# Linear attention with RMS norm and a SiLU feed-forward: other starting addresses for TensorE's operands

## The chip, the cores and the metric

One core of a Trainium2 chip. The metric is the device time of one execution in microseconds. The engines are TensorE (PE in the profile, its weight loads PEld), VectorE (DVE), ScalarE (ACT), GpSimd (POOL) and SyncE (SP), which issues all loads and stores here. A matmul on TensorE has two operands in the on-chip memory (SBUF): the stationary one, which it loads into its array ahead of the product, and the moving one, which it streams through it. Results go to PSUM.

## The reference

```python
kv  = einsum('bhsd,bhse->bhde', k, v)            # b 8, h 8, s 576, d 64
out = einsum('bhsd,bhde->bhse', q, kv)
x   = out / sqrt(mean(out * out, -1) + 1e-6) * g_norm
x   = x.transpose(0, 2, 1, 3).reshape(4608, 512)
h   = x @ w_in                                   # 512 x 2048
y   = (h / (1 + exp(-h))) @ w_out                # 2048 x 512
```

All in float32.

## The kernel before

The 4608 tokens are taken in nine tiles of 512 (t = 0 to 8), the 2048 hidden features in sixteen blocks of 128 (f). The attention of a batch element b (576 tokens, four pairs of heads) is done while TensorE works on the tile before the one that needs it, in jobs that are hung on fixed steps of the tile loop (`first_jobs`, `mid_jobs`, `last_jobs`). The order of all instructions is the order in which the program is written; nothing is rescheduled.

A float32 product is made of three products of rounded parts: each operand is an upper and a lower part (`gh` and `gl`, `wi[:, 0]` and `wi[:, 1]`, `qh` and `ql`), and lower by lower is left out. Nearly every matmul thus has a 128x128 stationary operand and 256 moving columns:

- `products` (through `halves`, line 479) makes the hidden layer of tiles 0 and 1: `wi` parts are stationary, x (`x_part`) moves. It writes `hp`.
- `product` (line 645) does the same for tiles 2 to 8, where a scheme of Strassen and Winograd's kind makes a pair of blocks from seven products. Stationary are `wi` parts or sums of them, moving are `x_second`, `operand4`, `operand5`, `operand6`. A pair of blocks takes 42 matmuls in two stretches, 24 and 18, that mostly follow each other.
- `project` (through `halves`, line 479) is the second layer: `gh` and `gl` are stationary, `w_out` parts (`wo`) move. It writes `acc` and, for a quarter of the last tile, `at`. A block f takes 24 matmuls, a pair 48.
- `mm_out` (lines 290 to 294) multiplies q by the state: `kh` and `kl` (or `kvm` in the plain form for b < 2) are stationary; q, or `qh` and `ql`, moves. It is done in two halves of the 576 tokens.
- `mm_kv` (line 257) makes the state from k (stationary) and v (moving), 64 columns at a time.

`pair_step` does a pair of blocks in tiles 2 to 8: 42 product matmuls, then the 48 project matmuls of the pair before. The q products of the next batch element stand between them in the first steps of a tile, four pairs of heads in two halves each; the k-v products stand in one block late in it.

Tiles live in pools. `const`, `weights`, `kvq`, `tmp`, `opool`, `small` and `gp` follow each other in SBUF in this order, and a pool gives its places out in the order in which the tags are first asked for. So a small unused tile (a "gap") at the head of a pool moves all behind it. In `weights`, places go to the tags `wo0` to `wo15` and `wi0` to `wi15`; at the start some of them hold k, v and q of the first batch element (`early`). `spare` and `late` give places in `const`: `x0` to `x2`, later `operand4` to `operand6` and the parts of the sums; and `x3`, `x32` and `wo_full`.

Of the kernel before, what the change touches and what calls it, by code (L numbers as in the profile page):

```python
# [8 lines left out]
F32 = mybir.dt.float32  # L9
# [21 lines left out]
def linear_attention_rms_silu_ffn(  # L31
# [23 lines left out]
    B, NP, P, S = q.shape  # L55
    D = P // 2
    DM = NP * P
    NF = w_in.shape[0]
    TN = 512
    NT = B * S // TN  # L60
    HS = S // 2
    LAG = 2
    WARM = 2

    const = ctx.enter_context(tc.tile_pool(name="const", bufs=1))
    weights = ctx.enter_context(tc.tile_pool(name="weights", bufs=1))
    kvq = ctx.enter_context(tc.tile_pool(name="kvq", bufs=8))
# [3 lines left out]
    gp = ctx.enter_context(tc.tile_pool(name="gp", bufs=LAG + 1))  # L71
# [2 lines left out]
    ps_at = ctx.enter_context(tc.tile_pool(name="ps_at", bufs=1, space=PSUM))  # L74
    dram = ctx.enter_context(tc.tile_pool(name="dram", bufs=1, space=bass.MemoryType.DRAM))

    gp.tile([P, 16], F32, name="gap_before_gated", bufs=1)
    kvm = [const.tile([P, P], F32, name=f"kvm{i}") for i in range(NP)]
    for t in kvm:
        nc.gpsimd.memset(t, 0.0)  # L80
# [4 lines left out]
    for i in range(4):  # L85
        nc.gpsimd.tensor_copy(
            out=both[32 * i:32 * i + 32, 32 * (i ^ 1):32 * (i ^ 1) + 32], in_=ident[32 * i:32 * i + 32, 32 * i:32 * i + 32]
        )


    warm_up = const.tile([P, 1], F32, name="warm_up")
    nc.gpsimd.memset(warm_up, 1.0)
    gcol = const.tile([P, 1], F32, name="gcol")
    d_eps = const.tile([P, 1], F32, name="d_eps")
    nc.gpsimd.memset(d_eps, float(D) * EPS)
    const.tile([P, 8], F32, name="gap")

    def load_g():
        for h in range(P // D):
# [7 lines left out]

    SHIFT = 48
    const.tile([P, SHIFT], F32, name="gap_before")
    x_second = const.tile([P, NP, 2, TN], F32R, name="x_second")
    x_first, lates = {}, {}

# [1 line left out]
        return const.tile(shape, dtype, name=name, tag=f"spare{n}")  # L118

    def late(n, shape, dtype, name):  # L120
        if not lates:
            const.tile([P, 64 - SHIFT], F32, name="gap_behind")
        if name not in lates:
            lates[name] = const.tile(shape, dtype, name=name, tag=f"late{n}")
        return lates[name]

    def x32(c, w):

        return late(c // 2, [P, 2, TN], F32, f"x32_{c // 2}")[:, c % 2, w]


    def block(kind, f, dtype):
        return weights.tile([P, 2, NP * P], dtype, name=f"{kind}{f}", tag=f"{kind}{f}")

    def load_block(kind, f):
        words[kind, f] = t = block(kind, f, I32)
        src = w_in.bitcast(I32)[f] if kind == "wi" else w_out.bitcast(I32)[f * P:(f + 1) * P, :]
        nc.sync.dma_start(out=t.rearrange("p a b -> p (a b)"), in_=src)
# [5 lines left out]
    def full_tile(kind, f):  # L144
        if kind == "wo":
            t = late(1, [P, 2, NP * P], F32, "wo_full")[:, f % 2]
        else:
            t = tmp.tile([P, S], F32, name="full", tag="tmp")[:, :NP * P]
        fulls[kind, f] = t
        return t  # L150
# [40 lines left out]
    def split_block(kind, f, upper):  # L191
        full = fulls.pop((kind, f))
        parts[kind, f] = w = block(kind, f, F32R)
        upper(out=w[:, 0, :], in_=full)
        nc.gpsimd.tensor_tensor(out=w[:, 1, :], in0=full, in1=w[:, 0, :].bitcast(F32), op=ALU.subtract)  # L195
# [9 lines left out]
    def x_part(t, a, c):  # L205

        if t == 1:
            return x_second[:, c, a]
        if c not in x_first:
            kind = {"shape": [P, 2, TN], "dtype": F32R, "name": f"x{c}"}  # L210
            x_first[c] = spare(c, **kind) if c < 3 else late(0, **kind)
        return x_first[c][:, a]
# [20 lines left out]
    class Pair:  # L233
# [50 lines left out]

        def mm_out(self, half):

            self.w = w = slice(half * HS, (half + 1) * HS)
            self.ps = ps = at_bank()[:, :HS]
            if self.plain:
                nc.tensor.matmul(out=ps, lhsT=self.kvm, rhs=self.q[:, w], start=True, stop=True)  # L290
                return
            nc.tensor.matmul(out=ps, lhsT=self.kh, rhs=self.ql[:, w], start=True, stop=False)  # L292
            nc.tensor.matmul(out=ps, lhsT=self.kl, rhs=self.qh[:, w], start=False, stop=False)  # L293
            nc.tensor.matmul(out=ps, lhsT=self.kh, rhs=self.qh[:, w], start=False, stop=True)  # L294
# [174 lines left out]
    def at_bank(tag=None):  # L469

        at_tags.append(at_tags.pop(0))
        return ps_at.tile([P, 512], F32, name="at", tag=tag or at_tags[-1])
# [101 lines left out]
    def place(name, n, dtype):  # L574

        if name not in once:
            once[name] = block("wi", HF + 2 * n + 1, dtype).rearrange("p a (j n) -> p a j n", n=H)
        return once[name]
# [235 lines left out]
    with tc.manual_schedule():  # L814
# [4 lines left out]
        for item in ORDER.split():  # L819
            kind, n = item.rstrip("0123456789"), int(item.lstrip("wiopbg") or 0)  # L820
# [236 lines left out]
```

## Time and profile before

| | |
|---|---|
| median of 3 runs | 841.53 us (841.49 to 841.56) |
| the profiled execution | 841.74 us, its span 840.0 us |
| PE busy | 830.0 us, 99% of the span, 7518 records |
| DVE, ACT, POOL busy | 63%, 43%, 17% |
| DMA | 122.81 MB, queue q1 at 41.5% of 16 engines |

A profile row names a group by line, engine and operation, and by the tiles that it writes and reads (`acc<-wo,gh` writes `acc`, the moving operand is `wo`, the stationary one `gh`). "Busy" counts overlapping instructions once; the mean is of single instructions, from start to end, and longer than the spacing of two, since they are pipelined. The chain of waits that ended last is followed back from the end; where it stays on one engine it gives, for each stretch of equal work, start, duration and count, and the duration over the count is the spacing. Some rows of the program appear as several in the trace: a matmul on plain float32 data does.

### The profile page before, as it was taken

How to read it: one execution, taken by the hardware profiler on the slowest of the kernel's cores; microseconds unless marked ns; L12 is line 12 of the kernel's file. 1: busy time of each engine (PE TensorE's matmuls, PEld its weight loads, DVE VectorE, ACT ScalarE, POOL GpSimd, SP SyncE). 2: the span in 40 equal slices, each digit the busy share in tenths (PEclk: the TensorE clock that was granted, in tenths of full speed). 3: DMA queues.
4: the chain of work that ended last, by engine and by line, in shares of the span. 5: the costliest groups of instructions: out<-in, count | busy, mean ns of one | idle time of the engine just before them, and what ended most of it. 6: DMA issues, size and time to landing. Idle time of an engine off the chain costs nothing.

```text
span 840.0 us, 18181 instructions
## 1 busy us (share of the span) xinstructions
PE 830.0 (99%) x7518; PEld 823.1 (98%) x7518; DVE 529.3 (63%) x1027; ACT 358.5 (43%) x744; POOL 146.0 (17%) x142
## 2 busy tenths in 40 slices
PE   9989999999999999999999999999999999999998
PEld 8889999999999999999999999999999999999998
DVE  4886875888376567657666667656865664464332
ACT  4766554534453255325542355235532432243222
POOL 2776883423020002000200011001100000000000
PEclk9999999999999999999999999999999999999999
DMA  8779011337342634364424452444423342334331
GB/s 330 304 257 363 2 58 52 141 140 271 99 174 93 219 109 153 101 214 144 165 98 155 162 171 88 157 158 157 151 96 105 102 151 102 101 101 151 101 101 51
DMA packets 42435, 122.81 MB, mean 146 GB/s; under 512 B 4849, under 2 KB 5105, under 8 KB 42353
## 3 DMA queue, kind: packets, MB, share of 16 engines
q1 hardware_dynamic: 42352, 121.65, 41.5%
q8 instruction: 59, 0.97, 0.5%
q14 instruction: 24, 0.19, 0.1%
HBM read 103.81 MB, written 17.83 MB: 145 GB/s over the span
## 4 chain that ended last, share of the span: by engine, by line
PE 94%; DMA 4%; POOL 1%; issue 0%; ACT 0%; SPq 0%
PE acc L479 47%; PE hp L645 32%; PE hp L479 9%; PE at L257 2%; DMA wo<-in_moe_w_out 1%; DMA k<-in_k 1%; DMA v<-in_v 1%; PE at L293 1%; PE at L294 1%; PE at L292 1%; DMA early_wi<-in_v 1%; PE at L479 1%; DMA wi<-in_moe_w_in 1%; PE at L290 1%; POOL wo L195 0%
## 5 line engine op out<-in xcount | busy, mean ns | idle before, releaser
L479 PE MATMUL acc<-wo,gh 128*128 128x256 f32 x2272 | 360.8, 281 | 0.0
L479 PEld LDWEIGHTS acc<-wo,gh 128*128 128x128 f32 x2272 | 307.3, 189 | 1.0 <-POOL wo L195 0.3
L479 PE MATMUL acc<-wo,gl 128*128 128x256 f32 x1136 | 226.8, 280 | 0.5 <-POOL gl L498 0.5
L479 PEld LDWEIGHTS acc<-wo,gl 128*128 128x128 f32 x1136 | 174.1, 189 | 0.7 <-POOL gl L498 0.7
L645 PE MATMUL hp<-x_second,wi 128*128 128x256 f32 x1344 | 163.7, 277 | 0.0
L645 PEld LDWEIGHTS hp<-x_second,wi 128*128 128x128 f32 x1344 | 158.0, 188 | 0.0
L645 PE MATMUL hp<-operand,wi 128*128 128x256 f32 x1008 | 124.7, 277 | 0.0
L645 PEld LDWEIGHTS hp<-operand,wi 128*128 128x128 f32 x1008 | 119.9, 188 | 0.0
L279 POOL TENSOR_TENSOR ql<-q,qh 128x576 fp32r<-128x576 f32 x24 | 35.6, 1485 | 377.2 <-ACT qh L278 342.6
L696 ACT COPY wi<-hp 128x256 f32<-128x256 f32 x56 | 20.9, 373 | 143.0 <-PE hp L645 143.0
L654 ACT ACTIVATE gh<-gf 128x512 fp32r<-128x512 f32 x56 | 35.4, 633 | 93.5 <-DVE gf L709 80.4
L654 ACT ACTIVATE gh<-wi 128x512 fp32r<-128x512 f32 x56 | 35.5, 634 | 80.5 <-DVE wi L709 67.6
L697 DVE TENSOR_TENSOR gf<-hp,wi 128x256 f32<-128x256 f32 x28 | 11.9, 425 | 86.4 <-ACT wi L696 86.4
L697 DVE TENSOR_TENSOR wi<-hp,wi 128x256 f32<-128x256 f32 x28 | 11.9, 425 | 85.8 <-ACT wi L696 85.8
L479 PE MATMUL hp<-x,wi 128*128 128x256 f32 x360 | 46.4, 283 | 1.5 <-POOL wi L195 1.5
L479 PE MATMUL hp<-x_second,wi 128*128 128x256 f32 x384 | 46.7, 278 | 0.0
L479 PEld LDWEIGHTS hp<-x,wi 128*128 128x128 f32 x360 | 43.3, 188 | 2.4 <-POOL wi L195 1.7
L658 DVE TENSOR_TENSOR gl<-wi,gh 128x512 fp32r<-128x512 f32 x56 | 38.4, 686 | 11.1 <-ACT wi L655 11.1
L479 PEld LDWEIGHTS hp<-x_second,wi 128*128 128x128 f32 x384 | 45.3, 188 | 0.1
L658 DVE TENSOR_TENSOR gl<-gf,gh 128x512 fp32r<-128x512 f32 x56 | 39.1, 698 | 7.4 <-ACT gf L655 7.4
L698 DVE TENSOR_TENSOR wi<-hp,wi 128x256 f32<-128x256 f32 x56 | 23.9, 426 | 29.8 <-PE hp L645 29.8
L320 DVE SCALAR_TENSOR_TENSOR x<-o,gcol,yT 128x128 f32<-128x128 f32 (+7 forms) x52 | 40.8, 784 | 1.9
(142 smaller groups left out, 997.7 us busy)
## 6 DMA issues: line engine op xcount, KB each, us to landing
wi<-sums_in_dram SPq DMA_DIRECT2D x112, 512.0 KB, 3.3
out<-ob SPq DMA_DIRECT2D x35, 256.0 KB, 2.2
wi<-in_moe_w_in SPq DMA_DIRECT2D x16, 512.0 KB, 7.6
wo<-in_moe_w_out SPq DMA_DIRECT2D x16, 512.0 KB, 8.5
sums_in_dram<-sum_parts SPq DMA_DIRECT2D x16, 512.0 KB, 2.9
k<-in_k SPq DMA_DIRECT2D x28, 288.0 KB, 4.7
v<-in_v SPq DMA_DIRECT2D x28, 288.0 KB, 5.2
q<-in_q SPq DMA_DIRECT2D x28, 288.0 KB, 3.8
```

Of the source, the lines that this page charges most:

```text
L257: nc.tensor.matmul(out=self.kv[h], lhsT=self.k[rows, c, :], rhs=self.v[rows, c, :], start=(start and r == 0), stop=(stop and r == 4),)
L279: nc.gpsimd.tensor_tensor(out=self.ql, in0=self.q, in1=self.qh.bitcast(F32), op=ALU.subtract)
L290: nc.tensor.matmul(out=ps, lhsT=self.kvm, rhs=self.q[:, w], start=True, stop=True)
L292: nc.tensor.matmul(out=ps, lhsT=self.kh, rhs=self.ql[:, w], start=True, stop=False)
L320: nc.vector.scalar_tensor_tensor(out=to, in0=self.o[:, a:e], scalar=gcol, in1=self.yT, op0=ALU.mult, op1=ALU.mult)
L479: nc.tensor.matmul(out=to[:, at:at + 256], lhsT=stationary, rhs=moving[:, at:at + 256], start=start and at == 0, stop=stop and at == n - 256,)
L645: nc.tensor.matmul(out=out, lhsT=a_of(i, a, c), rhs=x[:, b, c], start=(n == 0), stop=(n == 5))
L654: nc.scalar.activation(out=gh, in_=x, func=AF.Silu)
L658: nc.vector.tensor_tensor(out=gl, in0=x, in1=gh.bitcast(F32), op=ALU.subtract)
L696: nc.scalar.copy(out=p1, in_=u)
L697: nc.vector.tensor_tensor(out=c1[:, low], in0=v, in1=p1, op=ALU.add)
L698: nc.vector.tensor_tensor(out=u2, in0=y, in1=p1, op=ALU.add)
```

## The change

It moves data in SBUF and nothing else, but for one cut. Gaps of other sizes stand at the head of `const`, `kvq` and `gp`; one stands between `w_out`'s and `w_in`'s places in `weights`, and `weights_places` asks for all places of that pool in a fixed order before anything else is loaded. The halves of q's 576 columns become 256 and 320 instead of 288 and 288, so that the second begins 1024 bytes behind the first and not 1152.

```diff
-    HS = S // 2
+    CUT = 256
...
-    gp.tile([P, 16], F32, name="gap_before_gated", bufs=1)
+    def gap(pool, size, name):
+        pool.tile([P, size // 4], F32, name=name, bufs=1)
+
+    def weights_places():
+        for kind in ("wo", "wi"):
+            for f in range(NF):
+                block(kind, f, F32)
+            if kind == "wo":
+                gap(weights, 64, "gap_weights")
+
+    gap(const, 128, "gap_first")
+    gap(kvq, 192, "gap_q")
+    gap(gp, 64, "gap_gated")
...
-    const.tile([P, 8], F32, name="gap")
+    gap(const, 96, "gap_x")
...
-    SHIFT = 48
-    const.tile([P, SHIFT], F32, name="gap_before")
...
-        if not lates:
-            const.tile([P, 64 - SHIFT], F32, name="gap_behind")
...
+    weights_places()
...
-            self.w = w = slice(half * HS, (half + 1) * HS)
-            self.ps = ps = at_bank()[:, :HS]
+            self.w = w = (slice(0, CUT), slice(CUT, S))[half]
+            self.ps = ps = at_bank()[:, :w.stop - w.start]
```

Where the operands of TensorE begin, in bytes modulo 256, as the pools give the addresses out in the two programs (the steps inside these tiles are multiples of 256 bytes; the matmuls are the program's, not the trace's records):

| matmuls | count | moving, before | stationary, before | moving, after | stationary, after |
|---|---|---|---|---|---|
| `project`: wo by gh, gl | 3456 | 0 | 64 | 192 | 0 |
| `product`: x_second, operand4 to 6 by wi | 2352 | 192 | 0 | 192 | 0 |
| `products`: x0 to x2, x_second by wi | 672 | 192 | 0 | 192 | 0 |
| `products`: x3 by wi | 96 | 0 | 0 | 192 | 0 |
| q by kh, kl or kvm, first half | 76 | 0 | 128 | 192 | 0 |
| q by kh, kl or kvm, second half | 76 | 128 | 128 | 192 | 0 |
| k-v, b of 1 and more | 280 | 0 | 0 | 192 | 192 |
| k-v, first batch element | 40 | 0 | 0 | 0 and 192 | 192 and 0 |

No instruction is added or removed, and none changes its place on its engine or its waits; the q products and ACT's two copies of each are 256 and 320 columns wide.

## The prediction

> **What bounds the kernel now.** I read the page's busy times first, then its groups, then the chain of waits stage by stage, and the timeline of single blocks last.
>
> ```profile
> span 840.0 us, 18181 instructions
> PE 830.0 (99%) x7518; PEld 823.1 (98%) x7518; DVE 529.3 (63%) x1027; ACT 358.5 (43%) x744; POOL 146.0 (17%) x142
> PEclk9999999999999999999999999999999999999999
> ...
> L479 PE MATMUL acc<-wo,gh 128*128 128x256 f32 x2272 | 360.8, 281 | 0.0
> L645 PE MATMUL hp<-x_second,wi 128*128 128x256 f32 x1344 | 163.7, 277 | 0.0
> ```
>
> TensorE is busy for 99% of the span at the full granted clock, with no idle time ahead of its large groups; the next engine, DVE, stands at 63%. So the kernel is as long as its stream of matmuls, and only the time from one matmul's start to the next one's can move it. The two groups have one shape (128x128 weights, 256 columns) but means of 281 and 277 ns. These overlap; the spacing is what counts, and the chain of waits gives it, as a block's time over its count (columns: start, us, what):
>
> ```profile
> 212.53 2.63 PE at L257 x80
> ...
> 215.95 2.24 PE hp L479 x19
> 218.19 5.66 PE acc L479 x48
> 223.84 4.78 PE hp L645 x42
> 228.62 2.83 PE acc L479 x24
> ...
> 248.95 2.06 PE acc L479 x18
> 251.01 0.13 PE at L292
> ...
> 251.41 2.07 PE acc L479 x18
> ...
> 253.86 1.41 PE acc L479 x12
> 255.28 4.78 PE hp L645 x42
> 260.06 5.65 PE acc L479 x48
> ...
> 301.79 2.63 PE at L257 x80
> 304.41 5.66 PE acc L479 x48
> 310.07 4.95 PE hp L645 x42
> ```
>
> Line 645, `product`, mostly takes 4.78/42 = 113.8 ns a matmul; line 479 into `acc`, `project`, takes 5.65/48 = 117.7. But neither is bound to its number: the product block at 310.07 takes 4.95/42 = 117.9, and the project block at 304.41 is fast once it has started, as the timeline shows (two windows, rows of 4 and 2 matmuls in turn):
>
> ```profile
> 260.60 0.64 PE L479 MATMUL acc<-wo,gh 128*128 128x256 f32 x4
> ...
> 264.84 0.64 PE L479 MATMUL acc<-wo,gh 128*128 128x256 f32 x4
> 305.15 0.62 PE L479 MATMUL acc<-wo,gh 128*128 128x256 f32 x4
> ...
> 309.23 0.62 PE L479 MATMUL acc<-wo,gh 128*128 128x256 f32 x4
> ```
>
> Between the first two starts lie 36 matmuls in 4.24 us, 117.8 ns each; between the other two 36 in 4.08 us, 113.3 each. The same instruction on the same operands' places has two speeds, and holds one for whole blocks. I call them fast and slow; a slow matmul costs 4.4 ns more.
>
> What flips them? Set beside the table of starting addresses: `product` moves at 192 and loads at 0, `project` moves at 0 and loads at 64. In the rows from 255.28 on, fast product is followed by slow project, and that by fast product again. At 304.41 project came out fast, and the product behind it, at 310.07, came out slow for all its 42. So a block keeps its speed inside one pair of places, whatever tile or PSUM bank it passes, and changes it where the pair changes. The change makes the pair (192, 0) everywhere.
>
> **The change, part by part.** The instructions and waits of every engine stay in the same order. Only addresses and the widths of the q products change.
>
> (1) All that is slow now. If every matmul were fast (48 in 5.44 us, 42 in 4.76, 24 in 2.72, 18 in 2.04, 12 in 1.36), the excess that goes is, stage by stage:
>
> ```profile
> 616.96 5.65 PE acc L479 x48
> ...
> 752.60 5.65 PE acc L479 x48
> ...
> 763.03 2.47 PE acc L479 x21
> 765.50 0.35 PE at L479 x3
> ...
> 831.28 4.95 PE acc L479 x42
> ```
>
> From 612 us to the end: 14 project blocks of 48 (first and last shown), 7 of 21+3+21+3 (first half-block shown), and the last 48: 22 x 0.21 = 4.6 us; the three slower matmuls at the head of each of 21 product blocks (4.78 against 4.76) add 0.4. Together 5.0.
> One period between two k-v blocks (212.53 to 301.79, 89.3 us), shifted to begin at 223.84: the 24 at 228.62, 0.11; two blocks of 12, 0.10; four of 48 like 260.06, 0.84; the 42 at 310.07, 0.19, and the 48 behind it, 0.21; eight of 18 at 0.02 to 0.03, 0.2; heads of product blocks, 0.1. That is 1.75. From 224 to 612 lie 4.35 periods: 7.6.
>
> ```profile
> 168.00 2.74 PE hp L479 x24
> 170.74 2.83 PE acc L479 x24
> ...
> 51.05 2.74 PE acc L479 x24
> ...
> 58.11 2.83 PE acc L479 x24
> ...
> 112.07 2.83 PE hp L479 x24
> ```
>
> Before 224 us: in tile 1 eleven project blocks of 24 at 2.83 (one shown), 1.2; sixteen hidden-layer blocks at 2.74 to 2.75, 0.4; the 19 and 48 slow ones from 215.95 on, 0.3. In tile 0 both kinds come in both speeds, as the last three rows show; from 47 us to 124 eleven blocks are slow (first and last of the plain ones shown), 1.2. Together 3.1.
> In all 15.7 us, if nothing is slow any more.
>
> (2) q halves. The three products of a half take 0.39 to 0.40 us together now (251.01 to 251.41 is 0.40), 0.130 to 0.133 each. At the fast spacing 256 columns take 0.113, and 320 at most 320/256 of that, 0.142: 0.255 a pair against 0.260 to 0.267. With 72 such pairs (eight groups of three in each of six tiles, two halves to a pair) that is 0.4 to 0.8 us; I take 0.6. ACT's two passes over a half grow or shrink by 32 columns:
>
> ```profile
> L298 ACT ACTIVATE sq<-at 128x288 f32<-128x288 f32 x56 | 22.9, 409 | 44.5 <-PE at L294 37.8 <-PE at L290 6.7
> L299 ACT COPY o<-at 128x288 f32<-128x288 f32 x56 | 22.1, 395 | 0.0
> L696 ACT COPY wi<-hp 128x256 f32<-128x256 f32 x56 | 20.9, 373 | 143.0 <-PE hp L645 143.0
> ```
>
> A copy of 256 columns takes 373 ns and one of 288 takes 395, so 22 ns a pass, up for one half and down for the other. The cover is the 18 matmuls, 2.06 us, between two halves, against some 0.85 us of ACT for the wider one. Nothing on the path; without that cover it would be 0.04 us a half.
>
> (3) k, v, q, w_out and the early loads now land at 192 instead of 0. No row shows a load that lands there. Nearest:
>
> ```profile
> wi<-sums_in_dram SPq DMA_DIRECT2D x112, 512.0 KB, 3.3
> ...
> sums_in_dram<-sum_parts SPq DMA_DIRECT2D x16, 512.0 KB, 2.9
> ...
> 22.27 7.86 DMA k<-in_k
> ...
> 30.14 6.38 DMA v<-in_v
> ```
>
> `sum_parts` stands at 192 and leaves in 2.9 us, no more than the 3.3 of a load that lands at 0. So the likely cost is nothing; but loads carry the chain for the first 36 us, and the ends are -1.7 and +1.7 us (the 0.4 between 3.3 and 2.9 is 12%, on the 14.2 us of k and v in the chain, either way). I take +0.2, near the row that shows no cost. Behind 224 us the loads lie beside TensorE's work.
>
> (4) What stays. A restart behind idle time or behind the k-v matmuls can still fall on the slow side: at 215.95 (192, 0) did, 19 in 2.24, and held it until the pair changed. In tile 0 eleven of its blocks are slow. For these, and a few slower matmuls at each head, I keep 1.8 us.
>
> Sum: 15.7 + 0.6 - 0.2 - 1.8 = 14.3 us off. The profiled execution took 841.74 us (its span 840.0), 0.2 above the median of 841.53; so 827.4 for such an execution, and 827 as a median.
>
> The Trainium skill, page "SBUF — State Buffer", section "Who interferes with whom", says that TensorE's two reads, of what it moves and of what it loads, have independent ports and that it never waits on anyone. By that the sum would be 0 and the time 841.5. The trace disagrees already: 113.3 and 117.8 ns for one instruction at the full clock.
>
> **The rivals.**
> (a) Slow for good. What makes a product fast again now is the change of pair after a slow project block (255.28 behind slow project, 223.84 behind the slow 48 at 218.19). With one pair everywhere nothing flips. If the state left by the last q products, near 610 us, is slow, some 1,940 matmuls stay slow to the end: +8.5 us where 5.0 was lost before; if the q products do that in each tile, 48 us (to the next k-v block) in five tiles add 9. That gives 827 + 17.5, about 844. If the k-v restarts are slow as well, all 5,200 matmuls from 212 us on are: 22.9 us, about 850. For it: (192, 0) has held the slow speed as long as it lasted (4.95 for 42). Against it: the same pair, entered fast, has never turned slow inside a block, the q products will have that pair too, and the restart at 304.41 was fast with fast work ahead of it, while that at 215.95 had slow work ahead (170.74 is the last kind of block before it). It decides from the eighth q group of tile 6 on, for there is no restart behind it.
> (b) Only the k-v restart turns slow. The q products of the next tile, 19 us later, set it right: 165 matmuls x 4.4 ns = 0.7 us in each of five tiles. 831.
> (c) The place isn't the cause, but what the operands are or how they were written, and project stays slow: 841.5, perhaps 841 by the q halves. This is also what the page's rule gives. Against it: the fast project block at 305.15.
>
> **How the numbers follow.** Fast nearly throughout: 0.62, 825 to 830, likeliest 827. Rival (b): 0.15, 829 to 834. Rival (a): 0.17, of it 0.10 near 844, spread over 840 to 848 by how many tiles it takes, and 0.07 near 850. Rival (c): 0.06. 0.2% is 1.7 us, about what a measurement can tell from no change. Faster 0.62 + 0.15 = 0.77; same 0.06 + 0.03 = 0.09; slower 0.14. The range runs from 824 (all 15.7 + 0.6 us off, and 1.4 of the loads' better end) to 842, which takes in (c) and the mild end of (a) and leaves out the rest of (a) and the tails; the likeliest case alone is 825 to 830.
>
> **What would show it.** Right: the chain has project blocks of 48 at 5.44 to 5.46 us after 612 us, product blocks of 42 at 4.76, groups L479 and L645 with equal means near 276, and the q products at 113 and 140 ns. Wrong: 5.65 for 48 in every stage (rival c); products of 42 at 4.95 in a row up to the end (rival a); a k-v block with slow work behind it up to the q products (rival b); the first 36 us longer, with k and v landing later (term 3).

## The result and the profile after

The changed kernel takes 828.04 us (median of 5, 827.72 to 828.51) beside 841.56 for the kernel before on the same chip: a ratio of 0.9839, 95% interval 0.9825 to 0.9854. In a later comparison it took 827.98 beside 841.67.

From its page, the busy times, the two large groups and one kind of store (line numbers are 9 higher than before: `halves` is 488, `product` 654, q 301 to 303, k-v 266, and the plain q products 299):

```profile
span 825.9 us, 18181 instructions
PE 815.1 (99%) x7518; PEld 808.5 (98%) x7518; DVE 527.6 (64%) x1027; ACT 358.4 (43%) x744; POOL 145.6 (18%) x142
PEclk9999999999999999999999999999999999999999
...
L488 PE MATMUL acc<-wo,gh 128*128 128x256 f32 x2272 | 353.6, 277 | 0.0
...
L654 PE MATMUL hp<-x_second,wi 128*128 128x256 f32 x1344 | 163.1, 276 | 0.0
...
sums_in_dram<-sum_parts SPq DMA_DIRECT2D x16, 512.0 KB, 3.0
```

TensorE's busy time fell from 830.0 to 815.1 and the span from 840.0 to 825.9, at the same clock and share. The means of `project` and `product`, 281 and 277 ns before, are now 277 and 276.

The chain of waits, at places that answer to those shown of before (start, us, what):

```profile
30.39 6.41 DMA v<-in_v
...
80.81 2.83 PE acc L488 x24
...
114.95 2.83 PE acc L488 x24
117.78 2.63 PE at L266 x80
120.40 2.94 PE hp L488 x24
123.34 2.72 PE acc L488 x24
...
232.01 0.11 PE at L301
...
232.35 2.04 PE hp L654 x18
234.40 0.14 PE at L301
234.54 0.15 PE at L302
234.68 0.14 PE at L303
234.83 2.05 PE acc L488 x18
...
298.40 2.63 PE at L266 x80
301.03 5.66 PE acc L488 x48
306.69 4.76 PE hp L654 x42
311.45 5.44 PE acc L488 x48
...
817.41 4.76 PE acc L488 x42
```

Project blocks of 48 now take 5.44 us (113.3 ns each) where they took 5.65, up to the last 42 in 4.76. The block at 301.03 stands behind the k-v products: its 5.66 has 0.22 of slower matmuls at its head, as the one at 304.41 had before, and what follows is fast. What stays slow lies in tile 0: from 77 us to the k-v products at 117.78 every block of 24 takes 2.83, one 2.88.

To account for all of it, I summed over each trace, from the starting times of the matmuls (1 ns steps), what each of 6,538 matmuls with 256 columns of rounded parts takes, from its start to the next one's, above 113.33 ns (heads of blocks included, q products apart; 38 more, with over 150 ns to the next start or at the end, are left out):

| | before | after |
|---|---|---|
| excess of the 6,538, all stages | 15.79 us | 2.50 us |
| up to 118 us | 1.58 | 2.15 |
| 118 to 224 us | 2.11 | 0.08 |
| 224 to 600 us | 6.86 | 0.27 |
| from 600 us | 5.24 | 0.01 |
| the 144 q products in halves, in 48 groups of three | 18.90 us | 18.60 us |

13.3 from the matmuls and 0.3 from the q products; another 0.35 us is that the stream's first such matmul starts that much earlier, a lead that it still has at 35 us. That makes 13.9 of the 14.0 us between the two profiled executions (841.74 and 827.72).

### The profile page after: what moved, and what is told of

It reads as the page before. It is cut to its first block, busy times and chain, and to the rows that moved or that the text cites. A ratio compares the mean times of both kernels' runs of the same rounds, so it can differ in the third digit from the quotient of the medians.

```text
span 825.9 us, 18181 instructions
## 1 busy us (share of the span) xinstructions
PE 815.1 (99%) x7518; PEld 808.5 (98%) x7518; DVE 527.6 (64%) x1027; ACT 358.4 (43%) x744; POOL 145.6 (18%) x142
## 4 chain that ended last, share of the span: by engine, by line
PE 94%; DMA 4%; POOL 1%; ACT 0%; issue 0%; SPq 0%
PE acc L488 46%; PE hp L654 32%; PE hp L488 9%; PE at L266 2%; DMA wo<-in_moe_w_out 1%; DMA k<-in_k 1%; DMA v<-in_v 1%; PE at L302 1%; PE at L303 1%; PE at L301 1%; DMA wi<-in_moe_w_in 1%; PE at L488 1%; DMA early_wi<-in_v 1%; PE at L299 1%; POOL wo L204 0%
## 5 line engine op out<-in xcount | busy, mean ns | idle before, releaser
L488 PE MATMUL acc<-wo,gh 128*128 128x256 f32 x2272 | 353.6, 277 | 0.0
L488 PEld LDWEIGHTS acc<-wo,gh 128*128 128x128 f32 x2272 | 302.1, 188 | 1.0 <-POOL wo L204 0.2
L488 PE MATMUL acc<-wo,gl 128*128 128x256 f32 x1136 | 222.9, 276 | 0.5 <-POOL gl L507 0.5
L488 PEld LDWEIGHTS acc<-wo,gl 128*128 128x128 f32 x1136 | 171.8, 188 | 0.7 <-POOL gl L507 0.7
L307 ACT ACTIVATE sq<-at 128x256 f32<-128x256 f32 (+1 forms) x56 | 22.9, 410 | 44.5 <-PE at L303 35.7
```

What stands on the lines that cost most here:

```text
L307: nc.scalar.activation(out=self.sq[:, self.w], in_=self.ps, func=AF.Square)
L488: nc.tensor.matmul(out=to[:, at:at + 256], lhsT=stationary, rhs=moving[:, at:at + 256], start=start and at == 0, stop=stop and at == n - 256,)
```

## The experiments

"Slow" and "fast" are the prediction's 117.8 and 113.3 ns. A pair is written (moving, stationary), starting places modulo 256. Three theories stood at the outset:

- **P, a phase.** Fast is 17 steps of 6.667 ns (113.33), slow is 53 thirds of one (117.78, since three such matmuls take 353.3 = 53 steps). A block of matmuls stands in a phase of some 6.667 ns rhythm. What can run fast is a *difference* of 192 between moving and stationary place; shifting both by 64 bytes shifts the fast phase by a quarter, 1.67 ns, and so a run flips where the pair changes.
- **V, the values.** Moving at 192, or stationary at 0, is fast in itself.
- **U, uniformity.** Any one pair throughout will do, since nothing flips.

The edits are to the changed kernel unless another is named.

**One pair, but (0, 64).** All tiles of `const`, `weights`, `kvq` and `gp` that a matmul reads move by 64 bytes:

```diff
-    gap(const, 128, "gap_first")
+    gap(const, 192, "gap_first")
```

> The changed kernel with everything TensorE reads moved on by 64 bytes: all moving operands at 0, all stationary ones at 64 modulo 256, so the pair that project had before, now in every stage. Theory P (phase): in both traces the fast matmuls of one pair of places start at one and the same phase of a 6.667 ns period, 17 of which make their 113.3 ns; from (192, 0) to (0, 64) that phase moves by 1.67 ns, a quarter. So the difference moving minus stationary (192) decides whether a pair can be fast, and one pair throughout keeps the phase: 826.5 to 830 us, like the changed kernel, project blocks of 48 at 5.44. Rival V (values): 192 and 0 are good places and 0 and 64 are not: slow everywhere, 117.8 ns a matmul, about 855. Rival U (uniformity): any one pair throughout will do: 826.5 to 830 as well.

827.78 us (ratio to before 0.9836, 0.9822 to 0.9851), the changed kernel's time. Moving at 0 and stationary at 64 was the slow project's pair before; alone in the program it is as fast as (192, 0), as its chain shows:

```profile
258.25 5.44 PE acc L488 x48
263.69 4.76 PE hp L654 x42
```

V falls.

**One pair, (0, 0).**

```diff
-            if kind == "wo":
-                gap(weights, 64, "gap_weights")
...
-    gap(kvq, 192, "gap_q")
-    gap(gp, 64, "gap_gated")
...
-    gap(const, 96, "gap_x")
+    gap(const, 160, "gap_x")
```

> The changed kernel with all moving and all stationary operands at 0 modulo 256: one pair throughout, but with difference 0. P: no phase suits both operands, every matmul is slow, 117.5 to 119 ns: 6,720 x 4.2 to 5.7 ns over the fast 825.5, so 853 to 864. V: slow too, about 855. U: fast, 826.5 to 830.

869.19 us, ratio 1.0327 (1.0310 to 1.0344): the same instructions in the same order, 41 us above the changed kernel. From its chain of waits (lines one lower):

```profile
223.65 5.76 PE acc L487 x48
229.41 5.04 PE hp L653 x42
```

Both are 120.0 ns a matmul, 18 steps of 6.667, and so it is in every stage, the heads of blocks apart. U falls. P was right on the direction and wrong on the size: I had allowed 4.2 to 5.7 ns above fast; a whole step, 6.67, came.

**Project back to (0, 64), the rest as changed.**

```diff
     def weights_places():
+        gap(weights, 64, "gap_head")
...
-            if kind == "wo":
-                gap(weights, 64, "gap_weights")
...
-    gap(gp, 64, "gap_gated")
+    gap(gp, 128, "gap_gated")
```

> The changed kernel with project alone put back to its places before: w_out at 0, gh and gl at 64; everything else stays at (192, 0), q cut at 256. P: both pairs can be fast, but every change between them shifts the phase that is asked for by a quarter period, so fast product is followed by slow project: back to 839.5 to 842, project blocks of 48 at 5.65, product blocks of 42 at 4.78, with a fast project block behind each k-v block and a slow product block behind that. V: all project slow, product fast throughout: 828 + 3456 x 4.4 ns = 843, with no slow product block. If the q halves, k and v carried the gain instead: about 828.

843.31 us, ratio 1.0021 (1.0012 to 1.0031), a little over P's range. Its chain has the flips of before again, behind the k-v products:

```profile
301.72 2.63 PE at L266 x80
304.34 5.66 PE acc L488 x48
310.00 4.95 PE hp L654 x42
```

The time alone would fit V's 843 as well. But a product block of 42 in 4.95 is slow at (192, 0), where V has it fast. With two pairs of equal difference, a block is fast or slow by what stood ahead of it.

**Project at (192, 64), and at (0, 0).** One edit each, so that only one operand of `project` is off:

```diff
-    gap(gp, 64, "gap_gated")
+    gap(gp, 128, "gap_gated")
```

> The changed kernel with gh and gl alone back at 64: project has the pair (192, 64), difference 128, all else (192, 0). P: no phase suits project, so its 3,456 matmuls are all slow, by 4.4 to 6.7 ns (117.8 as the usual slow ones, or 120.0 as in the kernel with everything at 0): 843 to 852, and no fast project block anywhere, not even behind a k-v block. If a change of pair were the only cost: about 841.

```diff
     def weights_places():
+        gap(weights, 64, "gap_head")
...
-            if kind == "wo":
-                gap(weights, 64, "gap_weights")
```

> The changed kernel with w_out alone back at 0: project has the pair (0, 0), difference 0, all else (192, 0). P: project at 120.0 ns, as every matmul of the kernel with everything at 0: 828 + 3456 x 6.67 ns = 851, with product fast again some matmuls behind each project block; 848 to 854. If a change of pair were the only cost: about 841.

845.28 us (ratio 1.0044, 1.0031 to 1.0058) and 848.86 (1.0088, 1.0073 to 1.0103), both in range. From the chains, product and project of the first kernel, then project of the second, whose product blocks take 4.78:

```profile
614.90 4.76 PE hp L654 x42
619.66 5.69 PE acc L488 x48
```

```profile
622.05 5.74 PE acc L488 x48
```

Product, whose pair is untouched, is fast; project takes 118.5 and 119.6 ns. Moving just one of project's operands loses all of the gain and more; both have to be moved, and together.

**One pair, (128, 0).**

```diff
-                gap(weights, 64, "gap_weights")
+                gap(weights, 128, "gap_weights")
...
-    gap(kvq, 192, "gap_q")
-    gap(gp, 64, "gap_gated")
+    gap(kvq, 128, "gap_q")
+    gap(gp, 128, "gap_gated")
...
-    gap(const, 96, "gap_x")
+    gap(const, 32, "gap_x")
```

> The changed kernel with all moving operands at 128 and all stationary ones at 0: one pair throughout, difference 128. P: not the difference that can be fast, so no fast block: 117.8 to 120.0 ns each, 853 to 870 us. If a difference of 192 is only the best of several that work: 827 to 832.

860.95 us, ratio 1.0229 (1.0215 to 1.0243), as P had it. From its chain:

```profile
626.17 4.99 PE hp L654 x42
631.15 5.70 PE acc L488 x48
```

118.8 ns each, for both. The starting times show neither of the two speeds here but a cycle of five matmuls, of 120, 119, 115, 118 and 121 or 122 ns: with this difference the stream does not settle. A difference of 64 throughout was not tried.

**The places without the cut.** Both halves of q have 288 columns again; the second begins at 64.

```diff
-    CUT = 256
+    CUT = 288
```

> The changed kernel with q's halves at 288 and 288 again: the second half then begins at 64 modulo 256 (pair (64, 0), difference 64). P: the second halves' 72 products lose the phase, 5 to 10 ns each, and it has to be found again behind them: 0.5 to 1.5 us more, 828.5 to 830; if it isn't found, a slow stretch of 2 to 48 us follows each of 24 second halves, up to 840. If the cut carried nothing: 828.0.

848.58 us, ratio 1.0081 (1.0066 to 1.0096), far outside of my 828.5 to 830, and above the 840 that I gave for a phase that isn't found again: slower than the kernel *before*. From its chain, at the first q groups of tile 1, around a k-v block, and in the last stage:

```profile
135.91 2.72 PE hp L488 x24
138.63 0.13 PE at L301
...
139.03 2.83 PE acc L488 x24
...
297.63 4.95 PE hp L654 x42
302.58 2.63 PE at L266 x80
305.21 5.65 PE acc L488 x48
310.86 4.76 PE hp L654 x42
315.62 5.44 PE acc L488 x48
...
636.83 4.95 PE hp L654 x42
```

Fast up to 138.63; one q group of 288 columns, and all that follows is slow, through further groups and tiles, up to the next k-v products; fast behind these (310.86, 315.62) until the next q group; and from the last q groups on slow to the end. 5,032 matmuls are slow (117 ns or more), 22.5 us of excess. This is the prediction's rival (a), in a kernel that differs by the cut alone.

**The cut without the places.** The kernel before, with halves of 256 and 320:

```diff
-    HS = S // 2
+    CUT = 256
...
-            self.w = w = slice(half * HS, (half + 1) * HS)
-            self.ps = ps = at_bank()[:, :HS]
+            self.w = w = (slice(0, CUT), slice(CUT, S))[half]
+            self.ps = ps = at_bank()[:, :w.stop - w.start]
```

> The kernel before with the cut alone: q's halves 256 and 320, all addresses as before (both halves of q then begin at 0). With e4, which had the new places and the old cut and took 848.6 us, this is the fourth corner of a square. P: the old places change the pair at every stage, and each change from slow project back to product finds the fast phase again, so whatever the cut does to the phase lasts a block or two: 839.5 to 843 us. If the cut carries some 20 us by itself, as between e4 and the changed kernel: 821 to 830.

842.64 us, ratio 1.0014 (1.0005 to 1.0022). Its q products take 18.92 us, before's 18.90; the excess of the others is 16.97 for 15.79, for example at this product block, 2.73 before:

```profile
243.35 2.83 PE hp L645 x24
```

So the change's two parts give, as medians:

| | halves 288, 288 | halves 256, 320 |
|---|---|---|
| places as before | 841.56 | 842.64 |
| places as changed | 848.58 | 828.04 |

Neither part gains by itself. The places alone cost 7.0 us, the cut alone 1.1, and both together bring 13.5.

**Another cut at 192.** 192 and 384 columns; the second half begins at 768 bytes, so both stay at 192.

```diff
-    CUT = 256
+    CUT = 192
```

> The changed kernel with q cut at 192 instead of 256 columns: 192 and 384, both halves still begin at 192 modulo 256. It tells the place of the second half from the width of the halves, which the cut at 288 changed together. If the place is what the cut has to keep: 827.5 to 829. If the width matters, since 320 columns alone shift the state in e9 and three of them in a row do not: a last group of a tile that leaves the slow state would hold it, as with 288 columns, 838 to 850 us.

830.13 us, ratio 0.9863 (0.9849 to 0.9876), about 1 above my range. From its chain:

```profile
232.35 0.09 PE at L301
232.43 0.11 PE at L302
...
232.66 2.08 PE hp L654 x18
234.74 0.17 PE at L301
...
235.25 2.04 PE acc L488 x18
```

The stream is fast again behind each group. What it loses, some 2 us, lies mostly in two places: the q products take 19.86 us for 18.60, since 192 columns take 0.09 to 0.11 and so hardly less than 256; and the first matmul behind each of the 24 groups of 192 takes 146 ns (the 18 in 2.08 for 2.04), 0.8 us in all, so that the excess is 3.12 us for 2.50. It is thus not the width of 256 that keeps the state. In the kernel with 288 the first group to turn it, at 138.63, begins at 192 like the others, so there it was the width and not the place. Whether its second half, at 64, would turn the state too isn't separated.

**What stays slow in tile 0.** If a group of other widths can turn the state, one extra product in tile 0 might turn it back. Ahead of block f = 9 and of f = 12, one matmul of 320 columns is added, whose result the next product overwrites:

```diff
                     hp = h_bank()
+                    if t == 0 and f in (9, 12):
+                        nc.tensor.matmul(
+                            out=hp[:, :320], lhsT=parts["wi", f][:, 0, 0:P], rhs=x_part(0, 0, 0)[:, :320],
+                            start=True, stop=True,
+                        )
```

> The changed kernel with two more matmuls of 320 columns in tile 0 (x0 by a w_in part, into the bank that the step's products then begin anew): ahead of the hidden layer of f = 9 and of f = 12, where the changed kernel runs slow from 78 us to the k-v block at 115. In the trace of e3 a group of 320-column products with slow work ahead was followed by fast work. P: one such matmul shifts the phase, the slow stretches end at 82 and at 99 us, which saves some 240 x 4.4 ns = 1.0 us for 2 x 0.15 us: 0.7 us off, 827.0 to 827.6. If one isn't enough to leave the slow state: 0.3 us more, 828.2 to 828.6.

827.77 us, ratio 0.9834 (0.9821 to 0.9848), a little over P's 827.0 to 827.6. Run beside it, the changed kernel again:

> The changed kernel again, to compare the one above with on the same chip: 827.7 to 828.5 us, slow from 78 us to 115 or at another place of tile 0, where restarts decide.

827.98 us, ratio 0.9837 (0.9823 to 0.9850): 0.2 between them, no difference that can be told from the times. The chain of the first tells more (the extra product is line 1006):

```profile
81.21 2.83 PE acc L488 x24
84.04 0.15 PE hp L1006
84.19 2.73 PE hp L488 x24
...
98.04 2.72 PE acc L488 x24
100.76 0.14 PE hp L1006
100.90 2.83 PE hp L488 x24
```

The first extra product turns slow into fast, the second turns fast into slow. So I kept only the first (`f == 9`):

> As e9, with the one extra 320-column matmul ahead of f = 9 alone. In e9's trace that one turned slow work fast, and the one ahead of f = 12 turned fast work slow, so a single 320-column product changes the state whichever it is. P: the twelve or so blocks of 24 from 84 us to the k-v block at 118 run at 2.72 instead of 2.83: 1.3 us off for 0.15: 826.5 to 827.2 us. If the restart at 95 us or chance decides instead: 827.7 to 828.3.

827.02 us (826.77 to 827.14), ratio 0.9824 (0.9811 to 0.9837), and its chain:

```profile
84.19 0.15 PE hp L1006
84.33 2.73 PE hp L488 x24
...
114.50 2.72 PE acc L488 x24
```

Fast from 84 us on; 200 slow matmuls are left of 490, and the excess is 1.21 us for 2.50, a gain of 1.3 less 0.15 for the extra product. The best of all kernels here, by some 1.0 us, with work added to the bounding engine. Its time and the changed kernel's were taken on two chips (before took 841.75 and 841.67), and the intervals of the two ratios overlap, so the 1.0 rests on the traces more than on the medians.

## Why the prediction was right, and where not

The forecast was 827.0, its likeliest case 825 to 830; 828.0 came, by the mechanism named. By its steps:

**(1) The slow matmuls.** Sized right in sum: 15.7 us forecast from blocks of the chain, 15.79 summed over the single matmuls. That the two lie so close is luck in part, for the stages were off both ways: 3.7 us for 3.1 before 224 us, 7.0 for 7.6 from there to 612, 5.1 for 5.0 behind. The 7.6 counted the slow 24 at 228.62 in each period, though in the later ones only the 48 at 315.02, counted as well, stands there. That the pair carries it was right as well: with two pairs the flips return (843.31), with one operand of `project` off it is slower than before (845.28 and 848.86). What the prediction lacked is *which* pairs: it spoke of one pair everywhere, and one pair everywhere also gives 869.19 and 860.95. Of the differences tried throughout, 192, 128 and 0, only 192 was fast, and both pairs of the kernel before, (192, 0) and (0, 64), already had it; it did not note that.

**(2) q halves: the term that was mis-sized.** As a price of the q products, 0.6 us was forecast and 0.3 came: the pairs of halves take 0.258 where I had 0.255, since the three of 320 columns came at 141.7, 146.7 and 146.6 ns, where I had at most 142 for each. The larger error is that I costed the cut as a small term of its own. With the new places it is worth 20.5 us (848.58 less 828.04), and without them -1.1. The step that failed is the sentence against rival (a), "the q products will have that pair too": I used it as a matter of the places and never asked what the product of 288 columns would leave behind. For the kernel in hand the q products left the stream fast, so the total held; in this point that was luck, since no row of before has products of 256 or 320 columns there.

**(3) The loads.** In the chain k and v take 8.13 and 6.41 us, for 7.86 and 6.38, and v ends 0.28 later (36.80 for 36.52), near the +0.2 taken. But TensorE's first rounded matmul starts 0.35 earlier, in the repeat 0.26 earlier, and in the kernel with one extra product 0.16 later. It costs nothing that stands out of this spread. `sum_parts` leaves in 3.0 us for 2.9.

**(4) What stays slow.** 1.8 us forecast, 2.50 measured, and 2.15 of it in tile 0 up to the k-v products at 117.78. There it is more than before (1.58): 40 us of slow blocks with nothing to rescue them, which is rival (a) inside one tile. In the kernel before, the six matmuls that move x3, at the end of each hidden-layer block of the tile, had the pair (0, 0): in the block at 106.57 us they break off the fast spacing of 113 and 114 ns with 120, 112, 117, 118, 119 and 120, and that tile keeps changing speed. The sum of the four terms was 14.3, the profiled executions differ by 14.0 and the medians by 13.5.

**Rival (a)** was priced well: 844, or about 850 with the k-v restarts slow, for 5,200 slow matmuls. The kernel without the cut has 5,032 of them and took 848.58, though by another way: its restarts were fast and its q products turned it. The condition was in the changed program too; what decided was the width of the q products, which the prediction did not name as the point. One argument against (a) fell: that a restart keeps the speed of the work ahead. At 117.78 slow work stood ahead, and behind the heads (2.94 for 24) came fast blocks (2.72).

**Rival (b)** did not occur: the blocks behind 301.03 are at 4.76 and 5.44. **Rival (c)** is refuted by the uniform kernels: the same instructions on other places took 827.8, 861 and 869. By the rule of the Trainium skill, page "SBUF — State Buffer", section "Who interferes with whom", that TensorE's two read ports are independent and that it never waits on anyone, all three would take one time; in this case they don't.

## What to carry to other kernels

Where one engine is busy for 99% and a group of equal instructions has two speeds, divide each block's time in the chain by its count and set it beside the operands' starting addresses: here 41 us, 5% of the kernel, hang on these alone. Try at least two uniform placements, since uniform was both the best and the worst of them; and look at what the few instructions of another width leave behind them, since one group of three set tens of microseconds of matmuls to the longer spacing. A part that seems to cost nothing should be tried without, and the others without it: here two parts that each lose made the gain together.

## What the runs showed of the hardware that was not expected

- Spacing of matmuls with 256 columns of rounded float32 and a 128x128 stationary operand, by moving minus stationary place modulo 256: with 192, 113.33 or 117.78 ns, by state; with 0, 120.00 ns (project and product alike in the uniform kernel); with 128, 118.7 ns on average, in a cycle of five.
- The first three are 17, 17 2/3 and 18 steps of 6.667 ns. In the trace of before, counted from the start of its span, the fast matmuls of (192, 0) start at 4.3 ns modulo 6.667 in the block at 265.71 us and at 4.0 in that at 375.80; those of (0, 64) at 5.9 in the block at 304.41 us and 5.7 in that at 393.64. The distance, 1.6 to 1.7 ns, is about a quarter of the step, as 64 bytes are of 256, and the shift of some 0.3 in between is common to both. That fits a fixed rhythm against which both operands are read; what it is no run shows, nor whether it is one.
- A state outlasts tiles, banks and other engines' work: slow from 78 to 118 us in the changed kernel, and from the first of the last q groups, at 594 us, to the end, some 250 us, in the one without the cut.
- A single matmul of 320 columns turned the state both ways; three in a row, as the q groups have, left fast work fast (no run with one pair has slow work ahead of them); three of 288 turned fast into slow and not back. No rule that I have gives all three, and that is left open, as is what decides the state behind the k-v products.
